# Turning double-precision weights into float32 with one ScalarE conversion and one VectorE shift-and-or, and three instead of six plain-float32 weight blocks

## The chip, the cores and the metric

The kernel runs on one core of one Trainium2 chip. The time is device microseconds of one execution, and the number quoted is the median of three runs.

## The reference, cut to what matters

```python
def _attn_ref(r, k, v, w, u):                    # 4 x 8 heads, 768 tokens, 48 wide
    for t in range(S):
        cur = einsum('bhd,bhe->bhde', u[None] * kt, vt)
        y[:, :, t] = einsum('bhd,bhde->bhe', rt, state + cur)
        state = wt[:, :, :, None] * state + einsum('bhd,bhe->bhde', kt, vt)
def _moe_ref(x, w_in, w_out):                    # x: 3072 x 384, d_ff 2048
    h = x @ w_in
    g = np.where(h > 0.0, h, np.exp(np.minimum(h, 0.0)) - 1.0)
    return g @ w_out
reference = _moe_ref(_attn_ref(...), w_in, w_out)
```

`w_in` and `w_out` reach the kernel as float64: they are products of a float32 array and a double-precision scalar. Their 64-bit words lie in DRAM as pairs of 32-bit words, and the kernel itself makes float32 of them.

## The kernel before, in words

**Attention.** The recurrence runs in 24 units: units 0 to 3 hold 128 tokens of one batch entry each, units 4 to 23 hold 64 tokens of two entries. VectorE scans the decays (`es`, `gs`), scales k and r by them (`rh`), makes the diagonal terms (`rkc` for units 0 to 3; `rk`, `rku`, `md` later), spreads them on a matrix (`sp`, for units 0 to 3 on ScalarE), masks the scores (`mk`), scales and updates the state (`sc`, `up`), and makes the low part of x (`xl`). TensorE makes diagonal sums (`pd`), scores (`s`, from unit 8 `tr` and `va`) and values (`v`). ScalarE copies results out of PSUM (`xf`, `xh`, `kt`, `md`). A unit's `s` needs its `rh` and, from unit 2 on, its `sp`.

**The two matrix products.** Tokens come in six chunks of 512 columns, d_ff in 16 blocks f of 128. A step n is one block on one stretch of columns: `g1` (three k-tiles into one PSUM bank), ELU as `r1`, `r2` on ScalarE and `stt` on VectorE, then `g2` into three accumulators. Steps 0 to 13 of chunk 0 are narrow, because their tokens come early: steps 0 to 3 have 128 columns (blocks 0 and 1), steps 4 to 7 are blocks 2 to 5 on the first 256 columns, steps 8 to 13 are blocks 0 to 5 on the other 256. From step 14 on a step has all 512 columns.

A product of fp32 accuracy is made in one of two ways. The first `K32` = 6 blocks keep in chunk 0 their float32 weights `w_f`, and TensorE multiplies plain float32: six instructions for each `g1` or `g2` (L251, L283). All other products split weight and operand into a high and a low fp32r part, and TensorE makes nine multiplications: high by high, high by low, low by high (L255, L286). That needs `wh` (ScalarE, L695) and `wl` (VectorE, L707) for the weights, and for `g2` also `gh` (ScalarE, L269) and `gl` (VectorE, L273). After chunk 0 the six plain blocks are split too (`wt` on ScalarE, `wl` on VectorE, `wh` as a cast on GpSimd, L703).

**The weight conversion.** For block f, `raw.f` loads 128 rows of 6144 bytes (L668). Then come four passes over 128x768 elements: `a` (ScalarE, L673, the high word times a power of two), `cs` (ScalarE, L678, the three bits that the low word gives), `cb` (VectorE, L688, shift and or) and `cc` (VectorE, L692, the sign).

**Order.** Each engine's order is written out by hand in `SEQUENCE`, one list for an engine and one for the SP queue that issues the loads. `holds` keep buffers safe: `hold(pool, taker, users)` makes a taker wait for the users of the buffer that it takes over. `FILL` names the places where idle multiplications (`warm`, L409) are put in front of TensorE's work until the first `g2`. The lists begin like this:

```python
PE="pd.0 s.0 pd.1 s.1 v.0 v.1 g1.0 g1.1 pd.2 g1.2 g2.0 g1.3 g2.1 s.2 g2.2 ..."
DVE="es.0 gs.0 rkc.0 es.1 rh.0 gs.1 rkc.1 mk.0 cb.2 rh.1 cc.2 cb.0 cc.0 mk.1 cb.1 cc.1 ..."
```

At the end `least`, `guard` and `verdict` decide whether the fast result may stand; if not, the function `general` computes all again, slowly.

Of the kernel before, what the change touches and what calls it, by code (L numbers as in the profile page):

```python
# [96 lines left out]
cb.11 stt.15 cc.11 gs.6 stt.16 gl.15 sc.5 sp.5 xl.4 cb.12 rk.7 rku.6 cc.12 gl.16 wl.11 stt.17 rh.5 up.4 cb.13 md.6 stt.18 gl.17 wl.12 cc.13 stt.19
rh.6 mk.5 sc.6 gl.18 wl.13 cb.14 gl.19 sp.6 cc.14 up.5 xl.5 rku.7 es.7 stt.20 md.7 mk.6 sp.7 gl.20 wl.14 gs.7 sc.7 xl.6 up.6 rh.7 stt.21 cb.15 gl.21
cc.15 rk.8 mk.7 stt.22 wl.15 rku.8 gl.22 md.8 es.8 xl.7 gs.8 stt.23 up.7 es.9 rk.10 gl.23 rk.9 stt.24 rh.8 stt.25 rku.9 gl.24 sc.8 gl.25 es.10 wl.0
gs.10 rku.10 stt.26 stt.27 sc.9 gl.26 gl.27 gs.9 md.10 md.9 stt.28 wl.2 wl.1 stt.29 gl.28 rk.11 gl.29 rh.9 mk.8 rh.10 stt.30 es.11 gs.11 wl.3 stt.31  # L100
gl.30 gl.31 xl.8 up.8 sc.10 mk.9 stt.32 rk.12 es.12 gl.32 stt.33 rh.11 rku.12 gs.12 stt.34 rku.11 gl.33 wl.4 md.12 es.13 xl.9 md.11 up.9 wl.5 sc.11
mk.10 gl.34 gs.13 stt.36 stt.35 gl.35 gl.36 rk.13 rk.14 xl.10 up.10 stt.37 sc.12 rku.14 rh.12 gl.37 mk.11 es.14 stt.38 rku.13 md.13 gs.14 md.14 xl.11
stt.39 gl.39 gl.38 mk.12 up.11 rk.15 stt.40 sc.13 rh.13 gl.40 stt.41 xl.12 stt.42 gl.41 rk.16 rku.15 es.15 up.12 stt.43 gl.42 rku.16 md.16 sc.14 gl.43
stt.44 gs.15 md.15 stt.45 gl.44 gl.45 rh.14 mk.13 stt.46 gl.46 stt.47 es.16 gl.47 stt.48 up.13 sc.15 mk.14 gs.16 xl.13 rh.15 gl.48 stt.49 es.17 rk.18
gl.49 stt.50 gl.50 gs.17 up.14 mk.15 stt.51 xl.14 gl.51 rku.18 stt.52 rh.17 rh.16 rk.17 gl.52 md.18 stt.53 up.15 gl.53 es.18 rk.20 xl.15 sc.16 stt.55
stt.54 rku.17 md.17 gl.55 gl.54 stt.56 gl.56 mk.16 sc.17 es.19 rku.20 stt.57 stt.58 rk.19 gs.19 gl.57 up.16 gs.18 gl.58 xl.16 stt.59 rh.18 gl.59 md.20
mk.17 stt.60 rh.19 sc.18 gl.60 rku.19 stt.61 md.19 es.21 mk.18 up.17 sc.19 xl.17 gl.61 stt.62 rk.21 rku.21 es.20 gs.21 gl.62 gs.20 stt.63 up.18 gl.63
xl.18 stt.64 stt.65 gl.64 mk.19 rh.20 stt.66 gl.65 es.22 gl.66 stt.68 sc.20 gs.22 stt.67 rh.21 gl.67 stt.69 gl.68 stt.70 up.19 xl.19 sc.21 gl.69 gl.70
mk.20 stt.72 stt.71 gl.71 stt.73 md.21 rk.22 gl.72 gl.73 mk.21 stt.74 stt.75 gl.75 xl.20 gl.74 rh.22 rku.22 es.23 stt.76 rk.23 md.22 stt.77 up.20
gl.76 gl.77 stt.78 gl.78 stt.79 sc.22 gl.79 gs.23 stt.80 rh.23 stt.81 gl.80 stt.82 gl.81 gl.82 stt.83 rku.23 up.21 md.23 gl.83 stt.84 sc.23 stt.85  # L110
gl.84 mk.22 xl.21 mk.23 stt.86 xl.22 gl.85 xl.23 gl.86 stt.87 gl.87 stt.88 gl.88 stt.89 stt.90 gl.89 gl.90 stt.91 stt.92 gl.92 gl.91 stt.93 gl.93
stt.94 stt.95 gl.94 gl.95 stt.96 stt.97 gl.96 stt.98 gl.97 stt.99 gl.99 gl.98 stt.100 stt.101 gl.101 gl.100 stt.102 least stt.103 gl.102 gl.103
# [7 lines left out]
a.14 kt.5 gh.19 cs.14 xh.5 r1.20 cs.15 r2.20 fl.1 wh.14 pc.7 kt.6 gh.20 r1.21 xh.6 a.15 r2.21 gh.21 r1.22 r2.22 kt.7 wt.0 wh.15 gh.22 xh.7 r1.23 r2.23  # L120
gh.23 fl.8 r1.24 r2.24 r1.25 pc.8 r2.25 pc.9 gh.24 out.0.0 gh.25 out.0.1 fl.2 out.0.2 r1.26 r1.27 r2.26 gh.26 r2.27 wt.1 r1.28 gh.27 fl.10 r2.28 pc.10
r1.29 fl.9 r2.29 kt.8 wt.2 gh.28 gh.29 r1.30 r1.31 wt.4 r2.30 r2.31 wt.3 xh.8 gh.30 gh.31 r1.32 r1.33 r2.32 kt.9 fl.11 r2.33 gh.32 pc.12 pc.11 r1.34
wt.5 xh.9 r2.34 gh.33 fl.12 r1.35 kt.10 gh.34 r1.36 r2.35 r2.36 gh.35 xh.10 gh.36 r1.37 r2.37 gh.37 r1.38 r2.38 fl.13 r1.39 kt.11 gh.38 pc.14 pc.13
# [946 lines left out]
```

## Time and profile before

| | |
|---|---|
| median of three runs | 497.07 us (496.35 to 497.35) |
| profiled execution: its time | 496.44 us |
| profiled execution: span of the profile | 494.7 us |
| TensorE busy | 485.8 us |
| VectorE busy | 351.0 us |
| ScalarE busy | 265.0 us |
| GpSimd busy | 40.9 us |

The span begins with the first instruction and ends with the last; 1.7 us of the execution lie outside of it. A matmul's busy time is longer than its distance to the next one, since matmuls overlap; the distance is what counts where they follow each other.

### The profile page before, as it was taken

To read this page: it belongs to the slowest core of one execution; us is meant where nothing else is said; L and a number is where in the kernel's file an instruction comes from. 1 tells how busy PE (TensorE), PEld (TensorE's weight loads), DVE (VectorE), ACT (ScalarE), POOL (GpSimd) and SP (SyncE) were. 2 spreads that over 40 slices of the span, in tenths; PEclk is the share of its full clock that TensorE was granted. 3 is DMA by queue.
4 is the path that set the end of the run, shared out by engine and by line. 5 is a ranking of instruction groups with operands and counts; after the bars stand their busy time and mean duration, and the time that the engine had idled before them with its cause. 6 is when DMAs were issued, how large, how long until landed. Compare 5 with 4: busy or idle time off the path is not lost.

```text
span 494.7 us, 12041 instructions
## 1 busy us (share of the span) xinstructions
PE 485.8 (98%) x5014; PEld 402.3 (81%) x5014; DVE 351.0 (71%) x525; ACT 265.0 (54%) x526; POOL 40.9 (8%) x57
## 2 busy tenths in 40 slices
...
PEclk9999999999999999999999999999999999999999
...
GB/s 279 349 233 208 210 211 259 183 102 52 111 161 75 156 67 152 161 64 142 67 188 82 166 109 164 135 8 68 57 175 8 0 82 11 64 1 0 1 0 69
DMA packets 45611, 57.27 MB, mean 116 GB/s; under 512 B 29168, under 2 KB 29296, under 8 KB 45552
## 3 DMA queue, kind: packets, MB, share of 16 engines
...
HBM read 45.42 MB, written 4.72 MB: 101 GB/s over the span
## 4 chain that ended last, share of the span: by engine, by line
PE 89%; DVE 5%; ACT 3%; issue 1%; DMA 1%; DVEq 0%; ACTq 0%
PE acc L286 36%; PE ph L255 36%; PE acc L283 3%; PE py L529 3%; PE ph L251 3%; PE px L549 3%; PE px L529 2%; PE px L600 2%; PE py L542 1%; ACT ams L497 1%; DVE gl L273 1%; ACT w_f L673 1%; ACT wraw L678 1%; PE py L479 1%; DVE k L455 1%
## 5 line engine op out<-in xcount | busy, mean ns | idle before, releaser
L259 ACT ACTIVATE m<-ph 128x512 f32<-128x512 f32 (+2 forms) x104 | 58.4, 565 | 106.0 <-PE ph L255 86.4
L265 DVE SCALAR_TENSOR_TENSOR m<-m,ph 128x512 f32<-128x512 f32 (+2 forms) x104 | 66.4, 642 | 67.1 <-ACT m L262 66.7
L255 PE MATMUL ph<-xh,w_l 128*128 128x512 f32 x270 | 105.3, 390 | 0.0
L286 PE MATMUL acc<-gh,w_l 128*128 128x512 f32 x268 | 104.7, 391 | 0.0
L273 DVE TENSOR_TENSOR gl<-m,gh 128x512 fp32r<-128x512 f32 x90 | 64.1, 717 | 50.0 <-ACT gh L269 49.5
L269 ACT CAST gh<-m 128x512 fp32r<-128x512 f32 x90 | 55.8, 621 | 71.7 <-PE acc L286 47.0
L255 PE MATMUL ph<-xh,w_h 128*128 128x512 f32 x180 | 71.7, 398 | 0.3 <-DVE m L265 0.3
L286 PE MATMUL acc<-gh,w_h 128*128 128x512 f32 x180 | 71.7, 399 | 0.0
L255 PE MATMUL ph<-xl,w_h 128*128 128x512 f32 x180 | 70.1, 390 | 0.0
L286 PE MATMUL acc<-gl,w_h 128*128 128x512 f32 x180 | 70.1, 389 | 0.0
L262 ACT ACTIVATE m<-m 128x512 f32<-128x512 f32 (+2 forms) x104 | 61.1, 598 | 1.4
L255 PEld LDWEIGHTS ph<-xh,w_l 128*128 128x128 f32 x270 | 50.7, 188 | 10.8
L286 PEld LDWEIGHTS acc<-gh,w_l 128*128 128x128 f32 x268 | 50.3, 188 | 10.8
L508 POOL TENSOR_SCALAR_AFFINE_SELECT ams<-md 64x512 f32<-64x512 f32 x32 | 27.4, 858 | 217.3 <-DVE md L469 117.8
L255 PEld LDWEIGHTS ph<-xh,w_h 128*128 128x128 f32 x180 | 33.8, 188 | 8.1 <-DVE m L265 0.8
L286 PEld LDWEIGHTS acc<-gh,w_h 128*128 128x128 f32 x180 | 33.8, 188 | 7.3
L255 PEld LDWEIGHTS ph<-xl,w_h 128*128 128x128 f32 x180 | 33.8, 188 | 6.7
L286 PEld LDWEIGHTS acc<-gl,w_h 128*128 128x128 f32 x180 | 33.8, 188 | 6.6
L255 PE MATMUL ph<-xh,w_g 128*128 128x512 f32 x90 | 35.5, 395 | 0.6 <-DVE m L265 0.6
L286 PE MATMUL acc<-gh,w_g 128*128 128x512 f32 x88 | 35.2, 401 | 0.0
L255 PE MATMUL ph<-xl,w_g 128*128 128x512 f32 x90 | 35.0, 389 | 0.0
L286 PE MATMUL acc<-gl,w_g 128*128 128x512 f32 x88 | 34.3, 389 | 0.0
...
## 6 DMA issues: line engine op xcount, KB each, us to landing
wraw<-in_wraw_dram SPq DMA_DIRECT2D x16, 768.0 KB, 6.7
...
```

The source lines that it names most:

```text
L251: nc.tensor.matmul(ph, w_f[f][:, 0, k], x_[2][:, k], start=(k == 0), stop=(k == NK - 1))
L255: nc.tensor.matmul(ph, w[f][:, 0, k], y[:, k], start=(k == n == 0), stop=(k == NK - 1 and n == 2))
L259: act(s["m"], s["ph"], AF.Relu, scale=-1.0)
L262: act(s["m"], s["m"], AF.Exp, scale=-1.0)
L265: stt_(s["m"], s["m"], -1.0, s["ph"], ALU.add, ALU.max)
L269: nc.scalar.copy(s["gh"], s["m"])
L273: nc.vector.tensor_tensor(s["gl"], s["m"], s["gh"].bitcast(F32), ALU.subtract)
L283: nc.tensor.matmul(a_, w_f[f][:, 1, m], fold(s, s["m"][:, a:b]), start=first, stop=final)
L286: nc.tensor.matmul(a_, w[f][:, 1, m], fold(s, g[:, a:b]), start=(first and n == 0), stop=(final and n == 2))
L508: nc.gpsimd.affine_select(out=am[rs, h].rearrange("t q p s -> t (q p) s"), in_=u_["md"][rs].rearrange("t q p -> t (q p)").unsqueeze(2).bro ...
L529: nc.tensor.matmul(u_["py"][32 * j:32 * j + 32, h, k], l, r, **flags)
L549: nc.tensor.matmul(pa[q][ts, p], u_["k"][rs, p, ts], u_["r"][rs, p, ts], start=each or p == 0, stop=each or (close and p == NP - 1))
```

## The change

The load shifts the rows by 16 bits: all but the first two bytes of a row land at the start of the buffer. The 16 top bits of a double then stand where a bfloat16 can be read, and ScalarE converts them to float16 into the high half of a word of `top` (one buffer). VectorE then shifts the remaining bits and ors them with `top`. `cs` and `cb` are gone. Numbers that are too large for this path are looked for: `big.f` takes the largest magnitude of `w_h[f]`, and `least` counts it in. `K32` is 3: blocks 3, 4 and 5 are split from the start, so twelve half-width `g1` and `g2` change from plain float32 to fp32r. `wx` (the late loads of w for a check of units 0 to 7) shares the buffers of `rk` and comes late. All sequences are new. `general` gets a conversion of its own, which does not run with these inputs.

```diff
+HUGE = 2.0 ** 120
-K32 = 6
+K32 = 3
-FILL = {("pd", 0): 15, ("s", 0): 6, ("pd", 1): 8, ("s", 1): 5, ("v", 1): 5, ("pd", 2): 1, ("g1", 2): 5}
+FILL = {("pd", 0): 15, ("s", 0): 6, ("pd", 1): 4, ("s", 1): 4, ("v", 1): 4, ("s", 2): 2, ("g1", 2): 2}
...
     PE=
+pd.0 s.0 pd.1 s.1 v.0 pd.2 g1.0 v.1 g1.1 s.2 g1.2 g2.0 g1.3 g2.1 g2.2 pd.3 g1.4 g2.3 v.2 g1.5 s.3 g2.4 g1.6 v.3 g1.7 g1.8 g2.5 g2.6 g1.9 g2.7 g1.10
+g2.8 g1.11 g2.9 g2.10 g1.12 s.4 g1.13 g1.14 g2.11 v.4 g1.15 g2.12 g2.13 g1.16 g2.14 g1.17 g1.18 g2.15 s.5 g1.19 g2.16 v.5 g2.17 g1.20 g2.18 g1.21 s.6
...
     DVE=
+es.0 gs.0 rkc.0 es.1 rh.0 gs.1 rkc.1 es.2 rh.1 mk.0 gs.2 rkc.2 cc.0 mk.1 rh.2 cc.1 es.3 stt.0 gs.3 xl.0 stt.1 cc.2 mk.2 cc.3 stt.2 rkc.3 xl.1 stt.3
+wl.3 rh.3 cc.4 es.4 gs.4 stt.4 wl.4 cc.5 mk.3 stt.5 wl.5 big.3 stt.6 sc.4 gl.5 xl.2 cc.6 gl.6 stt.7 es.5 gl.7 rk.4 rku.4 stt.8 gs.5 md.4 xl.3 stt.9
+cc.7 wl.6 stt.10 sp.4 cc.8 rh.4 stt.11 es.6 wl.7 stt.12 gl.11 cc.9 mk.4 gl.12 rk.5 gs.6 stt.13 wl.8 rku.5 sc.5 cc.10 gl.13 wl.9 stt.14 md.5 rh.5 gl.14
...
     ACT=
+md.0 pc.0 sp.0 pc.1 kt.0 a.0 md.1 sp.1 kt.1 xf.0 xh.0 up.0 md.2 a.1 r1.0 r2.0 sp.2 r1.1 pc.2 r2.1 a.2 xf.1 up.1 kt.2 pc.3 a.3 r1.2 r2.2 xh.1 r1.3 r2.3
...
     SP=
-ld_w.0 ld_k.0 ubd ld_w.1 raw.2 ld_k.1 raw.0 raw.1 ld_v.0 ld_v.1 raw.3 ld_k.2 ld_w.2 ld_w.3 ld_v.2 raw.6 raw.4 ...
+ld_w.0 ld_k.0 ld_w.1 ubd ld_k.1 ld_w.2 raw.0 ld_v.0 ld_k.2 raw.1 ld_v.1 ld_w.3 raw.2 raw.3 ld_k.3 raw.4 ld_v.2 ...
...
+def fetch(nc, raw, src):
+    nc.sync.dma_start(raw.bitcast(U16)[:, 0:8 * DM - 1], src.bitcast(U16)[:, 1:])
+def high_bits(nc, top, raw):
+    nc.scalar.activation(top.bitcast(F16)[:, 1::2], raw.bitcast(BF16)[:, 2::4], AF.Copy)
+def low_bits(nc, g, raw, top):
+    nc.vector.scalar_tensor_tensor(out=g.bitcast(U32), in0=raw[:, 0::2], scalar=13, in1=top.bitcast(U32), op0=ALU.logical_shift_right, op1=ALU.bitwise_or)
...
+    def largest(f):
+        nc.vector.tensor_reduce(tops[:, f:f + 1], w_h[f].bitcast(F32).rearrange("p i k c -> p (i k c)"), AX.X, ALU.max, apply_absolute_value=True)
...
-        add(("cb", f), "DVE", K["cv"], lambda f=f: conv_b(f), [("cs", f), ("a", f)])
-        add(("cc", f), "DVE", K["cv"], lambda f=f: conv_c(f), [("cb", f)])
+        add(("a", f), "ACT", K["a"], lambda f=f: conv_a(f), [("raw", f), ("const",)])
+        add(("cc", f), "DVE", K["cc"], lambda f=f: conv_c(f), [("a", f)])
+        add(("big", f), "DVE", K["big"], lambda f=f: largest(f), [("wh", f)])
...
+        hold("top", ("a", f), [("cc", f)])
```

## Rows read from the trace of the kernel before

**Rows 1.** The page: busy time of the engines, and TensorE's granted clock.
```profile
PE 485.8 (98%) x5014; PEld 402.3 (81%) x5014; DVE 351.0 (71%) x525; ACT 265.0 (54%) x526; POOL 40.9 (8%) x57
...
PEclk9999999999999999999999999999999999999999
```

**Rows 2.** Stretches of the span: busy time, granted clock, DMA share, GB/s.
```profile
0.00:31.00 31.00, 28.80 (x315) 26.83 (x316) 27.18 (x41) 22.02 (x58) 3.30 (x14) 1.00 0.96 306
31.00:100.00 69.00, 69.00 (x833) 57.37 (x833) 68.74 (x103) 52.75 (x103) 1.59 (x3) 1.00 0.66 209
100.00:160.00 60.00, 57.80 (x704) 46.17 (x703) 53.49 (x77) 34.77 (x67) 12.98 (x12) 1.00 0.37 99
```

**Rows 3.** The same view for the idle multiplications of L409 alone.
```profile
0.00:31.00 31.00, 13.46 (x90) 12.31 (x90) 1.00 0.96 306
```

**Rows 4.** The chain that ended last: start, duration, work.
```profile
58.12 1.29 PE ph L251 x6
...
79.03 4.08 PE acc L286 x18
...
488.55 1.08 PE px L286 x6
```

**Rows 5.** Groups of instructions by form: busy, mean ns, idle before.
```profile
L273 DVE TENSOR_TENSOR gl<-m,gh 128x512 fp32r<-128x512 f32 x90 | 64.1, 717 | 50.0 <-ACT gh L269 49.5
...
L450 DVE TENSOR_TENSOR_SCAN eg<-w,reset 112x520 f32<-112x520 f32 x20 | 25.5, 1274 | 0.7
L440 DVE TENSOR_TENSOR_SCAN eg<-w,reset 112x520 f32<-112x520 f32 x20 | 24.7, 1236 | 0.0
L584 DVE COPY_PREDICATED ams<-upper_h,px 64x512 f32<-64x512 uint32 x32 | 23.5, 735 | 2.4 <-PE px L549 2.0
...
L678 ACT ACTIVATE wraw<-wraw 128x768 uint32<-128x768 uint32 x16 | 14.7, 918 | 1.2 <-DMA wraw<-in_wraw_dram 1.2
...
L469 DVE TENSOR_REDUCE md<-rk 128x8 f32<-128x384 f32 x20 | 10.8, 546 | 0.2
...
L703 POOL CAST w_g<-wt 128x768 fp32r<-128x768 f32 x6 | 7.7, 1300 | 48.1 <-DVE w_l L707 34.7 <-DVE reset L449 13.4
```

**Rows 6.** VectorE in order of time, consecutive from 57.81: start, duration, instruction.
```profile
57.81 0.95 DVE L688 SCALAR_TENSOR_TENSOR wg<-wg,wraw 128x768 uint32<-128x768 uint32 x1
58.67 0.55 DVE L465 TENSOR_TENSOR rk<-rk,ub 128x384 f32<-128x384 f32 x1
59.14 0.55 DVE L650 TENSOR_TENSOR xl<-wide,xh 128x384 fp32r<-128x384 f32 x1
59.61 0.42 DVE L265 SCALAR_TENSOR_TENSOR m<-m,ph 128x256 f32<-128x256 f32 x1
59.94 0.96 DVE L692 SCALAR_TENSOR_TENSOR wg<-wraw,wg 128x768 uint32<-128x768 uint32 x1
60.81 0.69 DVE L502 TENSOR_TENSOR ams<-ident_h,md 128x512 f32<-128x512 f32 x1
61.41 1.22 DVE L455 TENSOR_TENSOR k<-k,eg 112x1024 f32<-112x1024 f32 x1
62.55 0.96 DVE L688 SCALAR_TENSOR_TENSOR wg<-wg,wraw 128x768 uint32<-128x768 uint32 x1
```

**Rows 7.** VectorE's `gs.1`, `stt.24` and a `rh` beside a GpSimd cast.
```profile
9.25 1.23 DVE L450 TENSOR_TENSOR_SCAN eg<-w,reset 112x516 f32<-112x516 f32 x1
...
120.77 0.69 DVE L265 SCALAR_TENSOR_TENSOR m<-m,ph 128x512 f32<-128x512 f32 x1 [0.25 <-ACT m L262]
...
144.72 1.67 DVE L455 TENSOR_TENSOR k<-k,eg 112x1024 f32<-112x1024 f32 x1
```

**Rows 8.** TensorE in order of time: the first block step, and `s.4`.
```profile
20.81 1.60 PE L251 MATMUL ph<-wide,w_f 128*128 128x128 f32 x12
...
63.91 0.55 PE L542 MATMUL py<-ident,k 112*128 112x112 f32 x4
```

**Rows 9.** DMA issues: size of one and median us to landing.
```profile
wraw<-in_wraw_dram SPq DMA_DIRECT2D x16, 768.0 KB, 6.7
```

More of the change, by code (lines that the diff above doesn't have):

```diff
@@ L92 @@
+g1.99 g2.96 g1.100 g2.97 g1.101 g2.98 g2.99 g1.102 g1.103 g2.100 g2.101 g2a.0 guard g2a.1 g2a.2 g2.102 g2.103
 """,
     DVE="""
-es.0 gs.0 rkc.0 es.1 rh.0 gs.1 rkc.1 mk.0 cb.2 rh.1 cc.2 cb.0 cc.0 mk.1 cb.1 cc.1 xl.0 cb.3 rkc.2 es.2 stt.0 gs.2 stt.1 rh.2 es.3 stt.2 cc.3 stt.3
-mk.2 gs.3 rkc.3 cb.6 cb.4 stt.4 rh.3 es.4 cc.4 cc.6 cb.5 stt.5 cc.5 mk.3 stt.6 wl.6 es.5 stt.7 cb.7 gs.4 cb.8 cc.7 stt.8 rk.5 cc.8 wl.7 stt.9 rk.4
-sc.4 rku.4 wl.8 stt.10 gs.5 md.4 xl.2 stt.11 xl.3 cb.9 rku.5 xl.1 stt.12 cc.9 sp.4 rh.4 cb.10 stt.13 md.5 cc.10 wl.9 stt.14 mk.4 rk.6 gl.14 wl.10 es.6
@@ L97 @@
[L97 to L112, printed above, removed]
@@ new lines @@
+rh.6 stt.19 up.5 rk.7 es.8 xl.5 rku.7 gl.19 wl.14 md.7 stt.20 sp.7 mk.6 gl.20 cc.15 stt.21 gs.7 rk.8 xl.6 up.6 rh.7 sc.7 wl.15 stt.22 es.9 mk.7 rku.8
+gl.21 md.8 sc.8 gs.8 gl.22 rh.8 xl.7 up.7 gs.9 stt.23 rh.9 gl.23 es.10 mk.8 stt.24 rk.9 stt.25 gs.10 gl.24 rku.9 gl.25 wl.1 stt.26 es.11 md.9 rk.10
+rh.10 sc.9 rku.10 gs.11 stt.27 gl.26 xl.8 big.15 md.10 gl.27 stt.28 es.12 up.8 sc.10 gl.28 rk.11 mk.9 rh.11 stt.29 rku.11 gs.12 es.13 rk.12 md.11 wl.0
+gl.29 xl.9 stt.30 mk.10 rh.12 stt.31 rku.12 gs.13 up.9 es.14 gl.30 gl.31 md.12 rh.13 stt.33 stt.32 mk.11 gl.32 sc.11 rk.13 gs.14 big.11 xl.10 gl.33
@@ new lines @@
+es.15 big.6 stt.34 up.10 stt.35 gl.34 sc.12 rku.13 wl.2 gs.15 stt.36 md.13 rk.14 gl.35 big.8 rku.14 xl.11 rh.14 up.11 big.7 md.14 sc.13 stt.37 mk.12
+es.16 gl.36 big.2 gl.37 gs.16 stt.38 rh.15 gl.38 xl.12 es.17 up.12 stt.39 stt.40 gl.39 gl.40 mk.13 rk.15 sc.14 stt.41 gs.17 stt.42 rh.16 up.13 rk.16
+gl.41 rku.15 sc.15 md.15 rku.16 stt.43 xl.13 mk.14 gl.42 md.16 big.10 es.18 rk.17 big.1 big.13 gl.43 rku.17 big.12 xl.14 stt.44 gs.18 up.14 mk.15
+md.17 gl.44 stt.45 rh.17 rk.18 stt.46 gl.46 big.5 gl.45 es.19 mk.16 big.4 big.14 up.15 rku.18 xl.15 stt.47 md.18 rk.19 stt.48 gs.19 gl.47 big.9 rh.18
@@ new lines @@
+gl.70 mk.22 gl.71 stt.73 stt.72 rh.23 up.21 gl.72 gl.73 stt.74 gl.74 big.0 sc.23 stt.75 stt.76 xl.21 gl.75 gl.76 stt.77 gl.77 stt.78 gl.78 stt.79
+stt.80 gl.80 gl.79 stt.81 stt.82 gl.81 mk.23 stt.83 gl.82 xl.22 stt.84 gl.83 stt.85 xl.23 gl.84 stt.86 gl.85 gl.86 stt.87 gl.87 stt.88 stt.89 gl.88
+gl.89 stt.90 stt.91 gl.90 gl.91 stt.92 gl.92 stt.93 gl.93 stt.94 gl.94 stt.95 stt.96 gl.95 stt.97 gl.97 least gl.96 stt.98 gl.98 stt.99 gl.99 stt.100
+stt.101 gl.100 gl.101 stt.102 stt.103 gl.102 gl.103 end.1 verdict end.2 end.3
@@ L120 @@
[L120 to L123, printed above, removed]
@@ L132 @@
-xh.23 fl.7 r2.87 gh.87 r1.88 r2.88 out.4.0 out.4.1 gh.88 out.4.2 r1.89 r2.89 gh.89 r1.90 r2.90 gh.90 r1.92 r1.91 r2.91 gh.91 r2.92 gh.92 r1.93 r1.94
-r2.93 r2.94 gh.93 r1.95 gh.94 r2.95 gh.95 r1.96 fl.23 r2.96 gh.96 r1.97 r2.97 gh.97 r1.98 r2.98 r1.99 r2.99 gh.99 gh.98 r1.101 r1.100 r2.101 r2.100
-gh.101 gh.100 r1.102 r1.103 r2.102 r2.103 gh.102 gh.103 end.0 part
+md.0 pc.0 sp.0 pc.1 kt.0 a.0 md.1 sp.1 kt.1 xf.0 xh.0 up.0 md.2 a.1 r1.0 r2.0 sp.2 r1.1 pc.2 r2.1 a.2 xf.1 up.1 kt.2 pc.3 a.3 r1.2 r2.2 xh.1 r1.3 r2.3
@@ L339, in rwkv_elu_kernel @@
     ones = kp.tile([P, P], F32, name="ones")
-    ones_c = ones[0:R2, 0:1]
+    ones_c = ones[:, 0:1]
     big.tile([P, PAD], F32, name="pad")
@@ L370, in rwkv_elu_kernel @@
     raws, xts, held = {}, {}, []
+    top = cst.tile([P, 2 * DM], F32, name="top")
     def set_reset(eng, u_):
@@ L381, in constants @@
         nc.gpsimd.memset(pcs, 1.0)
+        nc.gpsimd.memset(flags, 0.0)
+        nc.gpsimd.memset(top, 0.0)
         make_identity(nc, ident)
@@ L711, in least @@
         nc.vector.tensor_reduce(low, pcs.rearrange("d u s -> d (u s)"), AX.X, ALU.min)
-        nc.vector.tensor_scalar(out=flags[:, NU:], in0=low, scalar1=2.0 ** -60, scalar2=None, op0=ALU.is_lt)
+        nc.vector.tensor_scalar(out=flags[0:R2, NU:NU + 1], in0=low, scalar1=2.0 ** -60, scalar2=None, op0=ALU.is_lt)
+        most = kp.tile([P, 1], F32, name="most")
+        nc.vector.tensor_reduce(most, tops, AX.X, ALU.max)
+        nc.vector.tensor_scalar(out=flags[:, NU + 1:], in0=most, scalar1=HUGE, scalar2=None, op0=ALU.is_ge)
     def guard():
-        units[0]["pf"] = pf = single()[0:1, 0:NU + 1]
+        units[0]["pf"] = pf = single()[0:1, 0:NU + 2]
         nc.tensor.matmul(pf, ones_c, flags, start=True, stop=True)
@@ L909, in rwkv_elu_kernel @@
             hold("pa", ("s", i), ends(i), fifo=False)
+    for i in range(LATE):
+        hold("rk", ("ld_wx", i), [("fl", i)])
     for f in range(NF):
@@ L923, in rwkv_elu_kernel @@
         add(("clear", w), "POOL", 0.5, lambda w=w: clear(w), done + [("v", i) for i in range(B, STACK) if (3 + i % 3) // 2 == w])
-    add(("least",), "DVE", 0.5, least, [(n, i) for i in range(NU) for n in ("fl", "pc")])
+    add(("least",), "DVE", 0.5, least, [(n, i) for i in range(NU) for n in ("fl", "pc")] + [("big", f) for f in range(NF)])
     add(("guard",), "PE", 0.2, guard, [("least",)])
```

148 lines of the change are left out of this document (75 added, 73 removed).

## The prediction, made before the changed kernel was run

> **What bounds the kernel now.** I read the page first, for the share of each engine: TensorE is busy 485.8 of 494.7 us at the full granted clock, 2.4 GHz, in every slice, VectorE 351.0 [rows 1]. That is an average over unlike stages, so I went to the stretches [rows 2]. Between 31 and 100 us TensorE is busy 69.00 of 69.00 us and VectorE 68.74: both are full. Before 31 us TensorE is busy 28.80, but 13.46 of that are idle multiplications [rows 3], so 15.7 us of the start (13.46 + 2.20 idle) are lost for the product. From 100 to 160 TensorE idles 2.2 us and VectorE 6.5. The chain [rows 4] consists of matmuls almost all the way. So a gain can come from three places: the start, fewer matmul microseconds, and the waits between 100 and 160. VectorE time is worth something only up to about 120 us, where VectorE is as full as TensorE.
>
> **Conversion passes.** `cs` on ScalarE goes, 16 x 0.918 = 14.7 us [rows 5]. ScalarE has room (22.02 of 31, 52.75 of 69 us [rows 2]), so I count that as nothing; without that room it would be 0.9 us a block. `cb` on VectorE goes: an instruction of this kind takes 0.95 us and moves the next start by 0.86 [rows 6], since neighbours overlap by about 0.09. The new `cc` has the same type, length and stride, 0.95. The new `a` has no row, because none writes 16-bit numbers at a stride. Below it cannot fall by more than its own 0.92, above I allow twice that. I take 0.92, the price of the nearest strided ScalarE pass. At twice that, four early `a` would add some 2 us to the start, the rest would find room on ScalarE.
>
> **`big`.** Sixteen new reductions over 768 elements. The one in the trace takes 0.546 for 384 [rows 5], so one of 768 lies between 0.55 and 1.09; I take 0.95, that of the other passes over 768. Together 15 us, which gives back what `cb` freed; but one alone (`big.3`) stands ahead of `s.4`, and the others come after 120 us.
>
> **Three plain blocks instead of six.** Twelve half-width products change. Plain float32 takes 1.29 us for one (six instructions) [rows 4]. The fp32r form is nine matmuls of 256 columns, which no row shows. At 512 columns one takes 4.08/18 = 0.227, at 384 columns 1.08/6 = 0.18 [rows 4]. So 256 columns cost at least half of the 512, 0.113, and at most 0.18; the straight line through both rows gives 0.133. I take 0.128, thus 1.15 for nine: 0.14 saved, 12 x 0.14 = 1.7 us. By the bounds it is 12 x (1.29 - 1.02) = 3.2 saved or 12 x (1.62 - 1.29) = 4.0 lost. Six narrow `gl` come on VectorE; by rows, 0.717 for 512 columns and a 256-column `stt` of 0.42 [rows 5, 6], I take 0.45, step 0.40.
>
> **The start.** VectorE's list is the clock here, since it runs almost without a gap. `gs.1` ends at 9.25 + 1.23 = 10.48 [rows 7], unchanged, because the list is the same up to there. Then come `rkc.1` 0.6, `es.2` 1.15, `rh.1` 1.14, `mk.0` 1.3, `gs.2` 1.4, `rkc.2` 0.6 and `cc.0` 0.9, all as steps: 17.6. So `g1.0` can start at 17.6 instead of 20.81 [rows 8]. Between old and new, one `v` (1.5 us) and one `pd` (1.0) have changed places ahead of it, so TensorE has lost 15.7 - 3.2 + 0.5 = 13.0 us instead of 15.7.
>
> Next, `s.4`, which waits for `rh.4`. I compared the two VectorE lists up to `rh.4`, which starts at 61.41 in the old [rows 6]. The new one lacks ten `cb` (8.6 us), one `cc` (0.87), `rk.5` and `rku.5` (0.94) and two narrow `stt` (0.66); it has one `wl` more (0.87), `big.3` (0.87) and three narrow `gl` (1.2). That is 8.1 us less: `rh.4` starts at 53.3 and `s.4` at 54.4 instead of 63.91 [rows 8]. Is TensorE there by then? Up to `s.4` it had 63.91 - 15.7 = 48.2 us of real work; without three half steps and `g1.14` that now come later (6.1) and with eight products cheaper by 0.14, 41.0. With 13.0 lost it arrives at 54.0. So the two meet, and `s.4` is 9.5 us early. But 5.5 us of work that the old order had done then (three half-width products at 1.15, one full step at 2.04) still lie ahead: TensorE is 4.0 us ahead, and `g2.13` brings 0.1.
>
> **The middle.** Does VectorE hold that lead? I compared the lists from `rh.4` to `stt.24`, which starts at 120.77 [rows 7]. The new one lacks six `cb` and two `rk` (6.1 us) and has 11.8 more: two `wl`, one `cc`, two `rh`, `es.10`, `gs.9`, `mk.8` (two instructions of 0.735 [rows 5]), `sc.8`, `rk.5`, `rku.5`, three `gl`, two `stt`. So `stt.24` comes at 53.3 + 59.4 + 5.7 = 118.4, or near 117 if waits that were among the old VectorE's 6.5 idle us [rows 2] vanish. TensorE alone would be there by 112: VectorE is the engine that sets the middle. It lets through 2.4 to 4 us, plus `s.8` (0.7) done by then. I take 3.9 of the 4.1. Behind this point VectorE is some 5 us ahead with later units, which about pays for the early ones of the fifteen `big`.
>
> GpSimd's casts fall from six to three. A `rh` beside one took 1.67 us [rows 7] where one without took 1.22 [rows 6], so three casts less are worth up to 1.35 us of VectorE. [...] I take 0.4 us of the 2.2 of TensorE's waits as saved; between 0 and all 2.2 is possible. The tail (`least` by two tiny instructions longer, `part` ahead of `end.0`) is beside TensorE's last matmuls and I take it as unchanged; uncovered it would be 0.5.
>
> **Sum.** 3.9 + 0.4 = 4.3. The profiled execution took 496.44, hence 492.1; the median of the runs is 0.6 above it, hence **492.8**.
>
> **The rivals.**
> *The lead is lost (no change).* VectorE's `big` and the new order bring back as waits in 120 to 200 what the start gained. For it: VectorE was 53.49 of 60 busy there. Against: `big` has no early taker and slack in the list. About 496.6.
>
> *The shifted load is slow (slower).* Rows begin two bytes off and are 6142 bytes long. In the first 31 us the DMA share is 0.96 at 306 GB/s [rows 2], so a load of 768 KB takes 2.6 us of the queue, and 6.7 to land [rows 9]. My walk has `raw.3` and `raw.4` with some 5 us to spare before `a.3` and `a.4`. At half rate four loads add 10 us, `raw.4` and all behind it come some 8 us late, and the start loses 8 where it gained 4: 501. It decides from about 4 us a load; up to 3.5 it is hidden. For it: the saturated queue, and no row with such a load. Against: a row stays one contiguous piece.
>
> *Narrow fp32r costs its upper bound.* 12 x 0.47 = 5.6 us over my price; some 3 are hidden where VectorE sets the pace: 495.5.
>
> *The clock falls.* Eight idle multiplications are gone from the start. The old start had granted clock 1.00 throughout [rows 2], with them. If a part of the start ran at 1.2 GHz, the 7 or so us of real work between 11 and 24 us would double, half of it in waits anyway: 3.5 lost, 496.3. Against: the new start is denser. The Trainium skill, TensorE: Matmul & The Clock Gate, Part 1, has idleness as what throttles the array; here no row shows it at 1.2 GHz, so what it takes is not known from this trace.
>
> *TensorE is never held in the middle.* All of the lead and all waits count, and the start is better than my walk by 2: 489.
>
> **How the numbers follow.** Forecast 0.58, its own range 490.5 to 494.5; never held 0.12; lead lost 0.10; slow load 0.08; narrow fp32r 0.07; clock 0.05. A measurement tells a change from none at about 0.2%, 1 us. The forecast, the better case, the narrow fp32r and half of the clock case lie below 496.1: faster 0.80. Most of the lost lead, same: 0.09. The slow load and what is left, slower: 0.11. The range leaves out the slow load, the tail of the better case and a little of the lost lead: 488.9 to 497.2, with both bounds of the fp32r price in it.
>
> **What would show it.** `g1.0` (L251 on 128 columns) near 17.6 and `s.4` near 54.4; the first full-width L255 near 57 instead of past 60; nine-matmul half steps of 1.15 us; `stt.24` near 117 to 118, with TensorE waiting for VectorE in 57 to 117; `big` at 0.95; `raw` landing in about 7 us; granted clock 1.00. Wrong would be: `cc` waiting for loads, `a` far over 1 us with `sp.2` late behind it, or ScalarE's queue waiting for the one `top` buffer while an `r1` stands behind it.

## The result and the profile after

The changed kernel takes 491.4 us (median of four runs, 491.0 to 492.1), the kernel before 496.7 beside it. The ratio is 0.9895, 95% interval 0.9875 to 0.9915: faster by 1.05%. The forecast was 492.8. The profiled execution took 491.04 with a span of 489.3, 5.4 less than before on both counts.

First the page of the changed kernel and its stretches (columns as in [rows 1] and [rows 2]); the last line is the same view for the idle multiplications alone, as in [rows 3].

```profile
PE 481.9 (98%) x5034; PEld 401.3 (82%) x5034; DVE 352.5 (72%) x533; ACT 258.5 (53%) x516; POOL 38.4 (8%) x56
...
0.00:31.00 31.00, 29.92 (x318) 28.16 (x318) 28.10 (x44) 21.69 (x61) 5.11 (x18) 1.00 0.93 304
31.00:100.00 69.00, 69.00 (x995) 59.24 (x995) 67.88 (x106) 49.98 (x98) 0.52 (x1) 1.00 0.68 215
100.00:160.00 60.00, 59.86 (x833) 48.32 (x832) 59.28 (x86) 31.48 (x66) 12.47 (x13) 1.00 0.51 133
...
100.00:136.00 36.00, 36.00 (x490) 29.27 (x489) 35.60 (x51) 20.03 (x42) 7.91 (x8) 1.00 0.50 132
...
0.00:31.00 31.00, 12.72 (x74) 11.66 (x74) 1.00 0.93 304
```

Read it against [rows 2, 3]. In the first 31 us TensorE lost 12.72 + 1.08 = 13.8 us instead of 15.7. From 100 to 160 it idles 0.14 us instead of 2.20, and none of that before 136. VectorE there is busy 59.28 instead of 53.49: the units come earlier and the reductions are new.

The chain of the changed kernel (start, duration, work), which answers to [rows 4], shows both kinds of half step side by side: plain float32 (six instructions, L262) and fp32r (nine, L266).

```profile
36.80 1.07 PE ph L266 x9
...
40.64 1.30 PE ph L262 x6
...
52.72 1.07 PE ph L266 x9
```

Groups by form, as in [rows 5]: the new `a`, `cc`, `big`, the narrow `gl` and the cast on GpSimd.

```profile
L230 ACT ACTIVATE top<-wraw 128x768 f16<-128x768 bf16 x16 | 17.3, 1084 | 0.1
L234 DVE SCALAR_TENSOR_TENSOR wg<-wraw,top 128x768 uint32<-128x768 uint32 x13 | 12.4, 951 | 0.1
L709 DVE TENSOR_REDUCE tops<-w_h 128x1 f32<-128x768 f32 x13 | 12.2, 942 | 0.0
L702 POOL CAST w_g<-wt 128x768 fp32r<-128x768 f32 x3 | 3.8, 1272 | 24.3 <-DVE reset L464 12.7 <-DVE w_l L706 11.5
L284 DVE TENSOR_TENSOR gl<-m,gh 128x256 fp32r<-128x256 f32 x6 | 2.5, 414 | 0.0
```

In order of time, the places that the prediction named, as in [rows 6 to 8]: `g1.0`, `s.4` and the start of `g1.24` on TensorE, then `rh.4` and `stt.24` on VectorE.

```profile
17.95 0.92 PE L262 MATMUL ph<-wide,w_f 128*128 128x128 f32 x6
53.63 0.55 PE L557 MATMUL py<-ident,k 112*128 112x112 f32 x4
111.35 0.50 PE L266 MATMUL ph<-xh,w_h 128*128 128x512 f32 x1
51.85 1.22 DVE L470 TENSOR_TENSOR k<-k,eg 112x1024 f32<-112x1024 f32 x1
116.45 0.69 DVE L276 SCALAR_TENSOR_TENSOR m<-m,ph 128x512 f32<-128x512 f32 x1
```

All five come earlier than before, `g1.24` by 5.9 us. Its start before the change, and in the changed kernel the start of `g1.26`, which takes over the PSUM buffer that `stt.24` gives free (`hold("ph", ...)`, two buffers):

```profile
117.24 0.39 PE L255 MATMUL ph<-xh,w_h 128*128 128x512 f32 x1
...
118.06 0.39 PE L266 MATMUL ph<-xh,w_h 128*128 128x512 f32 x1
```

TensorE's waits of the whole run, the changed kernel's list (what it waited for, us in total):

```profile
PE acc L424 <- POOL ones L390: 1.1, 1, 1.1
PE ph L266 <- DVE m L276: 0.5, 1, 0.5
```

The matmul of `guard`, close to TensorE's last work, and VectorE's last instruction, before and after:

```profile
486.76 0.21 PE L716 MATMUL py<-flags,ones 112*1 112x25 f32 x2
...
490.27 0.29 DVE L300 TENSOR_TENSOR o<-py,part 128x128 f32<-128x128 f32 x1
...
480.11 0.21 PE L721 MATMUL py<-flags,ones 128*1 128x26 f32 x2
...
483.69 0.29 DVE L311 TENSOR_TENSOR o<-py,part 128x128 f32<-128x128 f32 x1
```

`guard` starts 6.65 us earlier, yet the span is only 5.4 shorter. So 1.2 us are given back at the very end, the tail: VectorE's last instruction ends 4.16 us ahead of the end of the span before the change (490.56 of 494.72) and 5.35 ahead of it after (483.98 of 489.33).

### The profile page after: what moved, and what is told of

Its sections match the earlier page's. It is cut to its first block, busy times and chain, and to the rows that moved or that the text cites. A ratio compares the mean times of both kernels' runs of the same rounds, so it can differ in the third digit from the quotient of the medians.

```text
span 489.3 us, 12105 instructions
## 1 busy us (share of the span) xinstructions
PE 481.9 (98%) x5034; PEld 401.3 (82%) x5034; DVE 352.5 (72%) x533; ACT 258.5 (53%) x516; POOL 38.4 (8%) x56
## 4 chain that ended last, share of the span: by engine, by line
PE 94%; DVE 3%; DMA 1%; ACT 1%; issue 0%; SPq 0%; POOL 0%; DVEq 0%; POOLq 0%
PE ph L266 38%; PE acc L297 38%; PE py L544 3%; PE px L564 3%; PE acc L424 2%; PE px L544 2%; PE ph L262 2%; PE acc L294 2%; PE px L615 2%; PE py L557 2%; PE py L494 1%; DMA out_dram<-o 1%; DVE k L470 0%; DMA ams<-k 0%; DVE rk L480 0%
## 5 line engine op out<-in xcount | busy, mean ns | idle before, releaser
L266 PE MATMUL ph<-xh,w_l 128*128 128x512 f32 (+1 forms) x288 | 110.4, 383 | 0.0
L297 PE MATMUL acc<-gh,w_l 128*128 128x512 f32 (+1 forms) x286 | 109.8, 384 | 0.0
L284 DVE TENSOR_TENSOR gl<-m,gh 128x512 fp32r<-128x512 f32 (+1 forms) x96 | 65.1, 682 | 57.5 <-ACT gh L280 53.8
L280 ACT CAST gh<-m 128x512 fp32r<-128x512 f32 (+1 forms) x96 | 58.0, 606 | 70.7 <-PE acc L297 49.3
L297 PE MATMUL acc<-gh,w_h 128*128 128x512 f32 (+1 forms) x243 | 95.3, 392 | 0.0
L266 PE MATMUL ph<-xh,w_h 128*128 128x512 f32 (+1 forms) x243 | 94.9, 390 | 0.0
L297 PE MATMUL acc<-gl,w_h 128*128 128x512 f32 (+1 forms) x243 | 92.8, 382 | 0.1
L266 PE MATMUL ph<-xl,w_h 128*128 128x512 f32 (+1 forms) x243 | 92.8, 382 | 0.0
L266 PEld LDWEIGHTS ph<-xh,w_l 128*128 128x128 f32 x288 | 54.1, 188 | 10.8
L266 PEld LDWEIGHTS ph<-xh,w_h 128*128 128x128 f32 x243 | 45.7, 188 | 10.1 <-DVE m L276 0.7
L266 PEld LDWEIGHTS ph<-xl,w_h 128*128 128x128 f32 x243 | 45.7, 188 | 8.4
L455 DVE TENSOR_TENSOR_SCAN eg<-w,reset 112x520 f32<-112x520 f32 (+1 forms) x24 | 30.3, 1263 | 1.4 <-DMA w<-in_wkr_dram 1.4
L465 DVE TENSOR_TENSOR_SCAN eg<-w,reset 112x520 f32<-112x520 f32 (+1 forms) x24 | 30.2, 1258 | 0.8
L470 DVE TENSOR_TENSOR k<-k,eg 112x1024 f32<-112x1024 f32 x24 | 30.1, 1253 | 0.1
```

Of the source, the lines that this page charges most:

```text
L266: nc.tensor.matmul(ph, w[f][:, 0, k], y[:, k], start=(k == n == 0), stop=(k == NK - 1 and n == 2))
L280: nc.scalar.copy(s["gh"], s["m"])
L284: nc.vector.tensor_tensor(s["gl"], s["m"], s["gh"].bitcast(F32), ALU.subtract)
L297: nc.tensor.matmul(a_, w[f][:, 1, m], fold(s, g[:, a:b]), start=(first and n == 0), stop=(final and n == 2))
L455: nc.vector.tensor_tensor_scan(out=eg[:, 0, 0:n][:, ::-1], data0=u_["w"][:, 1:n + 1][:, ::-1], data1=reset[:, 0, 0:n][:, ::-1], initial=0. ...
L465: nc.vector.tensor_tensor_scan(out=u_["eg"][:, 1, 1:n + 1], data0=u_["w"][:, 0:n], data1=reset[:, 1, 0:n], initial=0.0, op0=ALU.mult, op1= ...
```

## The experiments

**Does VectorE set the middle?** Six of the late reductions are moved into 57 to 85 us, to give VectorE more to do there and TensorE nothing.

```diff
 DVE:
-stt.12 gl.11 cc.9 mk.4 gl.12 rk.5 gs.6 stt.13 wl.8
+stt.12 big.4 gl.11 cc.9 mk.4 gl.12 rk.5 gs.6 stt.13 big.5 wl.8
...
```

> The changed kernel with six reductions (big.4 to big.9, 5.2 us of VectorE steps) moved into 57 to 85 us, one behind each of stt.12 to stt.17. Predicted theory (VectorE's list sets the middle): stt.24 comes 5 us later and TensorE with it, of which the places that the six leave later give back 1 to 2: 494.5 to 496. Rival (VectorE runs ahead of TensorE there by the 0.8 to 5 us between a gl and its g2, and TensorE is not held): 491.4 to 492.4.

494.74 us (493.8 to 495.1), ratio 0.9953 (0.994 to 0.9966). The stretch of 57 to 100 us of this kernel, then `g1.24` and `stt.24`:

```profile
57.00:100.00 43.00, 40.05 (x576) 32.09 (x574) 42.88 (x65) 27.44 (x49) 0.00 (x0) 1.00 0.53 176
...
115.74 0.50 PE L266 MATMUL ph<-xh,w_h 128*128 128x512 f32 x1
...
121.00 0.69 DVE L276 SCALAR_TENSOR_TENSOR m<-m,ph 128x512 f32<-128x512 f32 x1
```

VectorE's `mk.5`, behind the six, comes 5.4 us later (83.63 against 78.20), and TensorE, which idled nowhere in this stretch, now idles 2.95 us; its `g1.24` is 4.4 later. So of 5.4 us of added VectorE work 4.4 arrive on TensorE: VectorE was not the bound of the changed kernel's middle, but it was 1.0 us away from being it. The time alone fits the predicted theory (494.5 to 496); it is the idle TensorE, which the changed kernel does not have, that tells the two apart. The 1.0 us is also the distance found at `stt.24` in the changed kernel: it ends at 117.14, 0.9 us ahead of `g1.26`.

**What do the reductions cost where they stand?** Once they are left out (with their task, and `tops` set to zero), once the six that stand between 130 and 185 us go behind 290.

```diff
...
-        add(("big", f), "DVE", K["big"], lambda f=f: largest(f), [("wh", f)])
...
```

> The changed kernel without the sixteen magnitude reductions (it leaves out the search for too large numbers); 14.9 us of VectorE less, 0.87 of it ahead of s.4. If VectorE's list sets the middle, as predicted: s.4 0.9 earlier and the waits of 136 to 147 and 172 to 181 gone, 489.5 to 490.3. If TensorE is never held in the middle and the reductions lie in gaps: within 0.5 of 491.4.

```diff
 DVE:
-gl.26 xl.8 big.15 md.10 gl.27
+gl.26 xl.8 md.10 gl.27
...
-gl.60 md.23 mk.20
+gl.60 big.15 md.23 mk.20
...
```

> The changed kernel with the six reductions that stand between 130 and 185 us (big.15, 11, 6, 8, 7, 2) moved behind 290 us; nothing is left out. If they take the time that VectorE lacks where it enters the chain at 136 to 147 and 172 to 181: 0.5 to 1.2 less, 490.2 to 490.9. If those waits come from the units' own chain (store, mask, values), no change: 491.2 to 491.6.

Without them 491.06 (490.9 to 492.1), ratio 0.9886 (0.9869 to 0.9903); late 490.54 (490.4 to 490.9), ratio 0.9871 (0.9855 to 0.9886). By the traces, which are finer than the times here, `guard` comes at 478.75 and 479.63 instead of 480.11: 1.4 and 0.5 us earlier. Up to 136 us both traces are that of the changed kernel within 0.2 us, so `big.3` ahead of `s.4` costs nothing. The stretch of 160 to 200 us in the changed kernel and with the late reductions:

```profile
160.00:200.00 40.00, 39.47 (x417) 32.35 (x416) 38.12 (x56) 19.21 (x39) 7.09 (x6) 1.00 0.60 147
...
160.00:200.00 40.00, 40.00 (x442) 32.73 (x444) 35.09 (x52) 19.50 (x40) 6.10 (x6) 1.00 0.58 148
```

The 0.53 us of idle TensorE are gone. So the "lead lost" rival is real as a mechanism, at 1.4 us, not as an outcome.

**Is it the conversion or the order?** Two exchanges. First the old four passes in the new order:

```diff
...
-        add(("a", f), "ACT", K["a"], lambda f=f: conv_a(f), [("raw", f), ("const",)])
-        add(("cc", f), "DVE", K["cc"], lambda f=f: conv_c(f), [("a", f)])
+        add(("a", f), "ACT", K["a"], lambda f=f: conv_a(f), [("raw", f)])
+        add(("cs", f), "ACT", K["cs"], lambda f=f: conv_low(f), [("raw", f)])
+        add(("cb", f), "DVE", K["cb"], lambda f=f: conv_b(f), [("cs", f), ("a", f)])
+        add(("cc", f), "DVE", K["cc"], lambda f=f: conv_c(f), [("cb", f)])
...
```

> The changed kernel (its order, three plain blocks, the reductions) with the conversion of before put back: unshifted load, cs right behind a on ScalarE, cb ahead of cc on VectorE, a third wg buffer in the place of top. Nine cb stand ahead of rh.4 and seven behind, up to stt.22. If VectorE's list is the clock of the start and the middle: rh.4 some 7 us later, stt.24 some 13 later, and TensorE follows except for the 2 us or so that it was behind VectorE: 501 to 504. If TensorE sets its own pace: below 494.

508.25 us (506.9 to 509.8), ratio 1.023 (1.015 to 1.031). Its `rh.4` comes at 61.91, 10.1 later, and its `stt.24` at 132.88, 16.4 later; TensorE is 15.2 to 16.5 behind from its 97 us on. VectorE is full (42.37 of 43 us in 57 to 100), TensorE is not:

```profile
31.00:57.00 26.00, 23.91 (x229) 21.32 (x230) 24.75 (x40) 20.10 (x46) 0.52 (x1) 0.93 0.61 211
57.00:100.00 43.00, 37.31 (x546) 30.34 (x545) 42.37 (x61) 32.69 (x57) 0.00 (x0) 1.00 0.47 158
```

Sixteen `cb` at 0.87 are 13.9 of the 16.4; the time is 4 us above what was expected. A wait of 1.97 us ahead of 31.5 was followed by a half step of 1.97 us from start to start (33.09 to 35.06) where 1.3 is usual, at a granted clock of 0.78 (31 to 36 us): this stall of TensorE cost more than its length.

Then the new passes in the old order: the old lists without `cs` and `cb`, six plain blocks and the old fillers; the `a` follow the order of the `cc`. ScalarE's list, against that of the kernel before:

```diff
 ACT:
-pc.0 md.0 pc.1 sp.0 a.2 cs.2 kt.0 a.0 cs.0 md.1 sp.1 a.1 cs.1 kt.1
+pc.0 md.0 pc.1 sp.0 a.2 kt.0 a.0 md.1 sp.1 a.1 kt.1
...
```

> The new conversion alone: the lists, the fillers and the six plain blocks of the kernel before, from which cs and cb are taken out; a follows the order of cc since there is one top buffer, the reductions stand behind gl.50 to gl.80, the late loads of wx at the end. If VectorE's freed time is what made the start shorter and the waits fewer: g1.0 two cb earlier, near 19, the waits of 100 to 160 gone, 493.5 to 495.5. If only the new order and the three blocks bring the gain: 496 to 497.5. If the one top buffer holds ScalarE up in the old order: above 498.

505.3 us (504.8 to 506.5), ratio 1.0171 (1.015 to 1.0191). Waits of ScalarE up to 60 us in this kernel:

```profile
ACT top L231 <- DVE w_f L235: 5.6, 4, 3.3
ACT top L231 <- DVE wg L235: 4.9, 2, 3.9
```

The third case: `a.0` waits in ScalarE's list for `cc.2` to free the one `top`, and `md.1`, `sp.1` and later the `r1` stand behind it. ScalarE loses 10.5 us, and VectorE is idle for 9.1 of the 26 us between 31 and 57 (busy 16.86). In the new order ScalarE has no such wait. In these lists, which were not made for it, the conversion is worth less than nothing. What it would bring in the old order with two `top` buffers was not tried.

**What are three plain blocks worth, and would two be better?**

```diff
-K32 = 3
+K32 = 6
...
```

> The changed kernel with six plain blocks (K32 = 6): gh and gl of steps 5 to 7 and 11 to 13 go, wh and wl of blocks 3 to 5 move behind chunk 0. By the half steps of the two profiles (1.29 plain, 1.07 as fp32r) TensorE has 12 x 0.22 = 2.6 us more; if TensorE's own work decides: 493.5 to 494.2. By the prediction's price of 1.15 it would be 1.7 more: 493.1. If VectorE decides, the six gl and three wl that are gone from its first 60 us (some 4.5 us) give that back: 491 to 492.

```diff
-K32 = 3
+K32 = 2
...
```

> The changed kernel with two plain blocks: block 2 is split from the start, its four half-width products become fp32r, wl.2 and two gl move into VectorE's first 50 us, wh.2 from GpSimd to ScalarE. TensorE has 4 x 0.22 = 0.9 us less; VectorE has 1.7 us more in a stretch where the reductions of early_big found 1.0 us of room. If both prices hold: 491 to 492, no gain. If TensorE's price alone decides: 490.3 to 490.7. If g1.4 has to wait for wl.2: above 492.

Six: 504.53 us (503.2 to 505.4), ratio 1.0146 (1.0063 to 1.0228), far more than any of the three cases. Up to `s.4` the run tells what was asked: eight of the twelve half-width products stand ahead of it, it comes 2.1 us later (55.70), TensorE idles 0.1 of the 26 us ahead of it while VectorE idles 6.65. So TensorE alone sets `s.4`, and 8 x 0.23 = 1.8 us is about the price. What follows comes from the blocks and the list together. In ScalarE's list `kt.4` stands behind `r1.13`, which waits for its buffer `m`: of a plain product `m` comes free only with its `g2`, of a split one already with `gl`. So TensorE waits 1.9 us for `kt.4`, and behind that comes a stretch at a lower granted clock (0.69), where a 512-column matmul takes 0.43 from start to start instead of 0.23 (`r1.13` on ScalarE, the stretch, two of the matmuls):

```profile
62.13 0.38 ACT L270 ACTIVATE m<-ph 128x256 f32<-128x256 f32 x1 [4.42 <-PE acc L294]
...
66.00:71.00 5.00, 5.00 (x17) 4.03 (x17) 1.55 (x2) 0.11 (x1) 0.00 (x0) 0.69 0.51 161
...
66.63 0.63 PE L266 MATMUL ph<-xh,w_l 128*128 128x512 f32 x1
67.06 0.63 PE L266 MATMUL ph<-xh,w_h 128*128 128x512 f32 x1
```

Whether another list would keep six plain blocks without this wait was not tried.

Two: 495.8 us (495.2 to 496.1), ratio 0.9972 (0.9957 to 0.9987): a product waits, though not for `wl.2`. TensorE idles 2.7 us in 31 to 57, most of it in `g1.10`, block 2 on the later columns:

```profile
PE ph L266 <- DVE xl L665: 1.5, 1, 1.5
```

A split block needs `xl` and `wl` early, which a plain one doesn't; 0.9 us of matmuls were bought with 1.7 us of VectorE, where the moved reductions, which stood somewhat later, had found 1.0 free.

**Is the shifted load slow?** The rows are loaded unshifted.

```diff
...
-    nc.sync.dma_start(raw.bitcast(U16)[:, 0:8 * DM - 1], src.bitcast(U16)[:, 1:])
+    nc.sync.dma_start(raw, src.bitcast(U32))
...
```

> The changed kernel with the rows of the weights loaded whole and unshifted (6144 bytes); ScalarE reads the high 16 bits where they then lie, VectorE shifts the wrong word, so the low bits of the weights are wrong; types, strides and lengths of all passes stay. If the shift costs nothing: 491.2 to 491.7 and a landing time of 7.7 us. If it costs queue time: landing near 6.7 as before, and up to 1 us less.

491.72 us (491.2 to 492.0). Landing of the unshifted rows in this run, and of the shifted in the changed kernel (KB, median us):

```profile
wraw<-in_wraw_dram SPq DMA_DIRECT2D x16, 768.0 KB, 8.3
...
wraw<-in_wraw_dram SPq DMA_DIRECT2D x16, 767.8 KB, 7.7
```

The shift costs nothing. The longer landing than in [rows 9] goes with the lists: in the run with the old order the shifted rows landed in 6.5.

**Does the clock need the idle multiplications?**

```diff
-FILL = {("pd", 0): 15, ("s", 0): 6, ("pd", 1): 4, ("s", 1): 4, ("v", 1): 4, ("s", 2): 2, ("g1", 2): 2}
+FILL = {}
```

> The changed kernel without any idle multiplication (FILL empty). If TensorE's clock stays at 1.00 in the start: 491.0 to 491.6. If the clock needs them, the granted clock of 0 to 31 us falls below 0.9 and the real work of the start takes longer: 493 to 497.

496.0 us (493.6 to 497.8), ratio 0.9985 (0.9953 to 1.0017). In order of time without fillers, the first `pd`, the first scores and `g1.0`; TensorE had done nothing before 7 us:

```profile
7.02 1.86 PE L494 MATMUL py<-ubd,rkc 112*128 112x2 f32 x8 [7.02 <-DVE rkc L489]
...
10.39 2.08 PE L564 MATMUL px<-k 48*128 48x128 f32 x16
...
21.88 1.63 PE L262 MATMUL ph<-wide,w_f 128*128 128x128 f32 x6
```

The same work takes 0.95, 1.16 and 0.92 in the changed kernel: without the fillers TensorE ran at half speed, the 1.2 GHz level, up to 25.2 us, and `guard` comes 4.3 us later. The granted clock reads 1.00 all that time in this run, so here only the durations show it. The Trainium skill, TensorE: Matmul & The Clock Gate, Part 1, has the throttled state as the default that activity releases; these durations agree.

**Where do the 1.2 us at the end go?** The seen difference is that `verdict` stands one place later in VectorE's list.

```diff
 DVE:
-gl.102 gl.103 end.1 verdict end.2 end.3
+gl.102 gl.103 verdict end.1 end.2 end.3
```

> The changed kernel with verdict one place earlier in VectorE's list, ahead of end.1. Theory (the program ends with TensorE's branch over general, which starts when verdict is done): verdict comes some 1 us earlier after the last matmuls and the tail of 5.35 us after the last VectorE instruction falls to about 4.2: 490.0 to 490.5 instead of 491.4. Rival (the last stores set the end): no gain, end.1 and its store come 0.35 later: 491.4 to 491.8.

491.77 us (491.0 to 492.2), ratio 0.9891 (0.9874 to 0.9908): no gain, the tail is 5.3. The theory falls: with `verdict` earlier, TensorE's branch now ends early, at 486.1, but the last store lands at 488.2, its issue held up by the one ahead of it, which took 1.54 us instead of 0.34; behind it ScalarE reaches the branch late and goes on only at 489.1. The next run, on top of the late reductions, has `least`, `guard` and `verdict` some 30 us earlier:

```diff
 DVE:
-gl.92 stt.93
+gl.92 least stt.93
...
-stt.97 gl.97 least gl.96
+stt.97 verdict gl.97 gl.96
...
 PE:
-g1.97 g2.95
+g1.97 guard g2.95
```

> late_big with least behind gl.92, guard behind g1.97 and verdict behind stt.97, so that the branch's register is loaded some 20 us before the end. If the late verdict costs tail: 5.15 us behind the last VectorE instruction become 4.2 to 4.6, 489.6 to 490.0. If the last store and TensorE's own arrival at the branch set the end: 490.3 to 490.8, as late_big.

491.08 us (490.3 to 491.4), ratio 0.9882 (0.9863 to 0.99), tail 5.2. Here VectorE and ScalarE are last: their first instruction behind the branch comes 3.9 and 3.2 us after it. The last run has the late reductions and a `general` without the conversion that the change gave it:

```diff
...
-            for f in range(NF):
-                raw = ld.tile([P, 4 * DM], U32, tag="raw", name="graw", bufs=1)
...
-                nc.vector.tensor_tensor(flat(w_l[f]), g, flat(w_h[f]).bitcast(F32), ALU.subtract)
...
```

> late_big without the conversion loop that the change added to general (it leaves out general's treatment of too large numbers, which does not run with these inputs), so that the engines jump over about as many instructions at the end as in the kernel before. Theory (the jump over a larger general is what the tail of 5.15 us after VectorE's last instruction is made of): TensorE's branch 3.4 instead of 3.9 us, the first instruction of VectorE and ScalarE behind their branches 0.5 instead of 3.2 to 3.8 us later, tail 4.2, 489.4 to 489.9. Rival (the landing of the last store sets the end): tail and time as in late_big, 490.3 to 490.8.

490.64 us (489.7 to 491.3), ratio 0.9864 (0.984 to 0.9888), tail 5.5. The instructions of the line with the branch (engine, kind, duration in ns, first and last start), first of the kernel before, then of the changed kernel, then of this one; the last SPq start is where the wait for the last store ends:

```profile
L948 SPq EVENT_SEMAPHORE  x8: 17/17/17, 490.6 to 493.4; - x8
L948 PEldq COMPARE_BRANCH  x1: 3384/3384/3384, 488.0 to 488.0; - x1
L948 DVEq EVENT_SEMAPHORE  x1: 21/21/21, 491.5 to 491.5; - x1
...
L950 SPq EVENT_SEMAPHORE  x8: 17/17/17, 486.3 to 488.0; - x8
L950 PEldq COMPARE_BRANCH  x1: 4107/4107/4107, 483.6 to 483.6; - x1
L950 DVEq COMPARE_BRANCH  x1: 72/72/72, 484.3 to 484.3; - x1
L950 DVEq EVENT_SEMAPHORE  x1: 21/21/21, 487.8 to 487.8; - x1
...
L950 SPq EVENT_SEMAPHORE  x8: 17/17/17, 486.4 to 488.2; - x8
L950 PEldq COMPARE_BRANCH  x1: 4387/4387/4387, 483.7 to 483.7; - x1
L950 DVEq COMPARE_BRANCH  x1: 72/72/72, 484.4 to 484.4; - x1
L950 DVEq EVENT_SEMAPHORE  x1: 21/21/21, 485.0 to 485.0; - x1
```

With the small `general` VectorE goes on 0.6 us after the start of its branch instead of 3.5, as expected, but TensorE's branch takes 4.4 us, not the expected 3.4, and the last store is waited for just as long, until 488.2. The time is the rival's. The Trainium skill, Runtime: NRT & Kernel Launch, Instruction fetch mechanics, says that a branch to a place not yet fetched waits for a fetch; the two VectorE rows agree with it. So three things end within about a microsecond of each other (TensorE's branch, the other engines' jump, the last store), and taking one away leaves the next.

In the kernel before, the store alone comes last: TensorE's branch had ended at 491.4 and VectorE gone on at 491.5. It was waited for until 2.76 us after its issue, in the changed kernel until 3.95 us after. The difference is the 1.2 us, although TensorE, VectorE and ScalarE go on there only 0.1 to 0.2 us sooner than that. By the packets in the traces the last nine of the store's 144 start only when a load of 16384 bytes on the instruction queue has ended: 484.67 to 486.09 in the changed kernel, 484.74 to 486.39 in the last run. This load starts 1.0 to 1.1 us after TensorE's branch; before the change it ran at 489.01 to 489.93, ahead of the store's issue at 490.60, and with the early `verdict` the store is done at 486.3. An early `verdict` and a small `general` together, as in the kernel before, were not tried; that they make up the 1.2 us is argued, not shown.

The best versions, the late reductions with and without the smaller `general` (490.5 and 490.6), are not told apart; the first is 0.9 us below the changed kernel by the medians, and its runs lie below all of that kernel's, but the intervals of the two ratios overlap.

## Why the prediction was right

The time came out 1.4 below the forecast and inside its own range. By its steps, on the span: forecast 4.3 us less, measured 5.4.

- **Passes.** `cc` 0.951 and `big` 0.942 as taken (0.95 each); the narrow `gl` 0.41 (0.45). `a` took 1.084, above the 0.92 but well below twice that, and ScalarE had room for it.
- **Half steps.** 1.07 instead of 1.15, plain 1.30: 12 x 0.23 = 2.8 us instead of 1.7. The matmul of 256 columns costs 0.119, nearer to half of the 512 than the straight line. With the waits and the tail this is one of the three terms that were mis-sized by over 1 us.
- **Start.** `g1.0` at 17.95 (17.6), TensorE lost 13.8 us (13.0), so 1.9 gained instead of 2.7. `rh.4` at 51.85 (53.3), `s.4` at 53.63 (54.4).
- **The middle, the step that failed.** "VectorE is the engine that sets the middle. It lets through 2.4 to 4 us": TensorE waited for nothing from 31 to 136 us, and all of its lead came through. That TensorE alone would reach step 24 by 112 was right (111.35), and `stt.24` was about where the walk put it (116.45; 117 to 118.4). The error was to hold `stt.24` against TensorE's arrival at step 24. What TensorE first needs of it is the buffer for `g1.26`, which stands in its list at 118.06, 0.9 us behind the end of `stt.24`; `g2.24` comes only at 122.14. The moved reductions show the same thin margin: 1.0 us of VectorE work was free, and the 5.4 us cost 4.4. In the sum this step weighed little, since 3.9 of 4.1 us were let through. The rival "never held" had the mechanism, with a chance of 0.12.
- **Waits.** 2.2 us before, 0.7 after (0.14 and 0.53 in the windows), so 1.5 saved instead of 0.4. A further 0.5 was to be had from the places of six reductions between 130 and 185 us, so VectorE time was worth something there too, not only up to 120.
- **Tail.** Taken as unchanged, 1.2 us longer.

The `rh` of 1.67 us in [rows 7] is not beside a cast. GpSimd at that time, before the change:

```profile
140.62 2.72 POOL L703 CAST w_g<-wt 128x768 fp32r<-128x768 f32 x2 [10.45 <-DVE w_l L707]
143.30 2.02 POOL L508 TENSOR_SCALAR_AFFINE_SELECT ams<-md 64x512 f32<-64x512 f32 x2
```

The casts end at 143.34; the `rh`, from 144.72, runs beside a spreading pass (`sp`, L508). No `rh` of the kernel before overlaps a cast, so the 1.35 us have no row behind them, nor have the 0.4 us of waits as far as they rest on it. Beside its six casts two other VectorE instructions ran 0.3 and 0.6 us longer than their like.

The sum on rows is 1.9 + 2.8 + 1.5 - 1.2 = 5.0 of 5.4; 0.4 is not accounted for. Errors of both signs, +1.1, +1.1, -0.8 and -1.2, nearly cancelled: the closeness of 492.8 is partly luck.

Of the other rivals the shifted load is refuted by the unshifted run, the upper price of narrow fp32r by its row. The clock did not fall with eight fillers fewer, by the durations (the first scores take 1.16 in both kernels); with none the price was 4.3 us, of the size that the prediction gave for it (3.5).
